# Attention and two MLPs in one planned program: four sums by DMA, a rule for urgent work, other due times, two outputs on a second queue

## The chip, the cores and the metric

The kernel runs on one core of a Trainium2 chip. The metric is the device time of one execution in microseconds (us), the median of three runs for the kernel before. A core has a matrix engine (TensorE, PE in the profile; PEld is its loading of weights), three other engines (VectorE, DVE; ScalarE, ACT; GpSimd, POOL) and SyncE (SP), which here only starts transfers. Each engine works its instructions off in the order in which the program lists them and waits where one needs a result that is not there.

## The reference

All values are fp32. With S = 768 positions, 8 heads of 64, 2 batches (1536 tokens), d_model 512 and d_ff 2048:

```python
def _attn_ref(q, k, v, n_sink, window):          # n_sink 4, window 128
    scores = scale * np.matmul(q, k.transpose(0, 1, 3, 2))
    keep = is_sink | in_window                   # first 4 keys, or the last 128 up to here
    scores = np.where(keep, scores, -1000000000.0)
    a = np.exp(scores - np.max(scores, axis=-1, keepdims=True))
    a = a / (np.sum(a, axis=-1, keepdims=True) + 1e-09)
    return np.matmul(a, v)

def _moe_ref(x, w_in, w_out):
    h = x @ w_in
    return (h * np.clip(h + 3.0, 0.0, 6.0) / 6.0) @ w_out

def _moe2_ref(x, w_in, w_out):
    h = x @ w_in
    return (h * (1.0 / (1.0 + np.exp(-1.702 * h)))) @ w_out

def reference(**kwargs):
    x = attention, with heads put beside each other: (1536, 512)
    return _moe2_ref(_moe_ref(x, moe_w_in, moe_w_out), moe2_w_in, moe2_w_out)
```

## The kernel before

**Arithmetic.** Every fp32 operand of an MLP product is split into a high and a low part (`xy`, `w0h`/`w0l`, `wg`), and a product is three matmuls: high by high, high by low, low by high. The high part is a cast (L444 on ACT, L446 on DVE), the low one a subtraction on DVE (L557 for weights, L572 for the gated values `g`, L1456 for the attention's output x).

**Tiles and stages.** The tokens are 12 tiles of 128. Attention goes by tile and by "duo" (half a tile's heads, 24 duos): 48 score matmuls (L1355), mask and row minimum (L1370, DVE), exponential (L1378, ACT), the inverse of the sums (L1386 and L1387, DVE), four scales (L1397 on DVE or L1395 on ACT, whichever the planner picks), transposes (L1406, 16 for a tile), a copy of what they left (`pts`, L446 or L444), values (L1429 and L1437, 48 for a tile), and the split of x (L444, L1456). An MLP's d_ff is cut into 16 weight tiles f. The packed weights of a tile are loaded by SP (`stage`, two buffers) and converted to fp32 in five steps: L474 on ACT, then L479, L487, L495 and L502 on DVE (the last two 1.2 us each). Up-products (L1132) give h; the gate is L1144 on ACT and L1149 on DVE; down-products are L1181.

MLP1 runs interleaved with attention, in blocks of 512 tokens by 8 weight tiles (first token 0, 512, 512 and 1024), up to about 259 us. The other half of its d_ff, for tokens 0 and 1024, is computed with seven half-size products instead of eight (L717, 336 matmuls of 256 columns; sums around them L734, L741, L750, L755), between about 259 and 325 us, beside MLP2's first block. These products need x in other combinations. `halve` makes them once all attention is done: it adds the high and low part of x back together (L806: two groups of tokens by four tiles = 8 additions of 128x512 on DVE), takes differences (L816) and splits them again (L826, L831). The 8 sums lie in 7 buffers, so the eighth reuses one. What follows, MLP2 in two similar schemes (L629, then L929), is the second half of the run.

**What sets the order.** `Plan.issue` emits the program. Each operation has modelled costs on the engines that may do it, and a due time; due times run backwards from the ends of blocks, whose pace is set by constants (`RAMP0`, `RAMP`, `PAIR`, `PAIR2`, `RATE`, `RATE2`). Of the engine that could start earliest, the planner takes from the operations that could start within `SLACK` = 50 ns of the earliest one the one that is due first:

```python
soon = min(c[0] for c in best[eng]) + SLACK
start, o, cost = min((c for c in best[eng] if c[0] <= soon), key=lambda c: c[1].due)
```

Where an operation may go to two engines, the planner takes the one on which it would end first, with a part of its cost added on each (`PACT` on ACT, `PDVE` on DVE). The order on each engine is fixed by this before the program runs.

**The end.** The last quarter of the output is four pieces, each an addition on DVE (L1052) and a transfer to memory issued by SP (`send`, L978).

Of the kernel before, what the change touches and what calls it, by code (L numbers as in the profile page):

```python
# [9 lines left out]
F32 = mybir.dt.float32  # L10
# [4 lines left out]
ALU = mybir.AluOpType  # L15
# [14 lines left out]
RATE_DMA = 340  # L30
# [3 lines left out]
NVB = 3  # L34
NVC = 3
SLACK = 50
ISSUE = 1300
ADD_DMA = 4500
PACT = 0.15
PDVE = 0.5  # L40
STRETCH = 1.0
LATER = 1000000
H_BANKS = 3
RAMP0 = 9000
RAMP = 1700
PAIR = 4300
PAIR2 = 5500
DOWN = 7000
START = 3000
RATE = 1.6  # L50
RATE2 = 1.25
NU = 3
NG = 2
PX = 8
# [14 lines left out]
def tile_sink_window_attention_moe_moe2(  # L69
# [71 lines left out]
    def load_vc(T):  # L141
# [5 lines left out]
    xyh, xyl = (  # L147
        [
            xy[:, :, (2 * s + k) * NC * 256 : (2 * s + k + 1) * NC * 256].rearrange("p a (c n) -> p a c n", c=NC)
            for s in range(NBLK)  # L150
        ]
        for k in range(2)
    )
# [80 lines left out]
    with tc.tile_pool(name="msk", bufs=1) as mp:  # L234
# [18 lines left out]
            out=out, in0=grid, scalar1=x, scalar2=LOW, op0=op, op1=ALU.mult  # L253
# [41 lines left out]
    class Plan:  # L295
# [70 lines left out]
        def issue(self):  # L366
# [22 lines left out]
            while ready:  # L389
                best = {}  # L390
                for o in ready:
                    placed = self.place(o)
                    if placed is None:
                        continue
                    t = placed[0]
                    pick = None
                    for eng, cost in o.opts:
                        x = max(t, at[eng])
                        for d in o.deps:
                            x = max(x, d.finish + self.lag(d.eng, eng))  # L400
                        score = x + cost * (1 + early[eng])
                        if pick is None or score < pick[0]:
                            pick = (score, x, eng, cost)
                    best.setdefault(pick[2], []).append((pick[1], o, pick[3]))
                assert best, "the plan is stuck"

                eng = min(best, key=lambda e: min(c[0] for c in best[e]))
                soon = min(c[0] for c in best[eng]) + SLACK
                start, o, cost = min((c for c in best[eng] if c[0] <= soon), key=lambda c: c[1].due)
                end = start + cost  # L410
                ready.remove(o)
                for b, n in zip(o.new, self.place(o)[1]):
                    b.slot = n
                    self.slots[b.cls][n] = b
                    b.tile = self.make[b.cls](b.slot)
                o.fn(ENG[eng])
                o.eng = eng
                if eng == "SP":

                    start = max(start, self.lanes.pop(0))  # L420
                    at[eng] = start + 400
                    self.dma_free = max(start + 600, self.dma_free) + cost
                    end = self.dma_free + LAND - 600
                    self.lanes.append(end + 300)
                elif eng == "POOL":
                    at[eng] = start + ISSUE
                else:
                    at[eng] = end
                o.start, o.finish = start, end
                self.end = max(self.end, end)  # L430
                for b in o.bufs:
                    b.left -= 1
                    b.free_at = max(b.free_at, end)
                for b in o.new:
                    if b.kind:
                        self.left[b.kind] -= 1
                for x in succ.get(id(o), ()):
                    need[id(x)] -= 1
                    if not need[id(x)]:
                        ready.append(x)  # L440
# [11 lines left out]
    def parted(x):  # L452

        return x.rearrange("p (a n) -> p a n", a=2)
# [54 lines left out]
    def plan_mlps(plan, blocks, item_due, late=None):  # L509
# [287 lines left out]
        def halve(t0, when):  # L797
# [4 lines left out]
            x = [[b for half in halves(t0, 512) for b in plan.x[half][c]] for c in range(NC)]  # L802
            for c in range(NC):
                plan.op(
                    [("DVE", 602)],
                    lambda e, c=c: e.tensor_tensor(  # L806
                        out=parted(full[c].tile), in0=xyh[s][:, :, c, :].bitcast(F32),
                        in1=xyl[s][:, :, c, :].bitcast(F32), op=ALU.add,
                    ),
                    when, reads=x[c], writes=[full[c]], after=plan.done,  # L810
                )

            def take(a, ac, b, bc, to, tc):
# [46 lines left out]
        def downs(t0):  # L860
# [107 lines left out]
                        when, reads=[x], writes=[y],  # L968
                    )

            def send(to, s, half, when):
                rows = out[s * 512 : s * 512 + 512, :].rearrange("(l q h) d -> q h l d", l=8, q=4)
                share = 4 // len(to)
                for e4 in range(4):
                    y = to[e4 // share]
                    plan.op(
                        [("SP", 131072 / RATE_DMA)],
                        lambda e, e4=e4, y=y: e.dma_start(  # L978
                            out=rows[e4][:, :, half * 256 : half * 256 + 256],
                            in_=y.tile[:, e4 % share * 256 : e4 % share * 256 + 256],  # L980
                        ),
                        when, reads=[y], chain="dma",
                    )
# [65 lines left out]
            for e4 in range(4):  # L1049
# [5 lines left out]
                    ),  # L1055
                    t3, reads=[bw[e4], u4[e4 // 2]], writes=[c12[e4]],
                )
            send(c12, 0, 1, t3)

        def operand(x):  # L1060

# [649 lines left out]
```

## Time and profile before

| | |
|---|---|
| median of 3 runs | 580.94 us (580.4 to 582.3) |
| profiled execution | 582.73 us |
| its span in the profile | 580.86 us |
| busy PE / DVE / ACT / POOL | 97% / 84% / 68% / 9% of the span |
| granted TensorE clock, mean | 0.987 |
| chain that ended last | PE 84%, DVE 10%, ACT 3%, DMA 1% |

The span is the time from the first to the last record of the profile; the 1.87 us around it belong to the execution as well. Busy time of PE is modelled: a matmul of 512 columns is shown as 0.38 us long while the next one starts 0.216 us after it, so a row of PE that reads as busy may still hold short idle times.

### The profile page before, as it was taken

How to read it: one execution, taken by the hardware profiler on the slowest of the kernel's cores; microseconds unless marked ns; L12 is line 12 of the kernel's file. 1: busy time of each engine (PE TensorE's matmuls, PEld its weight loads, DVE VectorE, ACT ScalarE, POOL GpSimd, SP SyncE). 2: the span in 40 equal slices, each digit the busy share in tenths (PEclk: the TensorE clock that was granted, in tenths of full speed). 3: DMA queues.
4: the chain of work that ended last, by engine and by line, in shares of the span. 5: the costliest groups of instructions: out<-in, count | busy, mean ns of one | idle time of the engine just before them, and what ended most of it. 6: DMA issues, size and time to landing. Idle time of an engine off the chain costs nothing.

```text
span 580.9 us, 11878 instructions
## 1 busy us (share of the span) xinstructions
PE 562.5 (97%) x4626; PEld 499.3 (86%) x4626; DVE 489.1 (84%) x1065; ACT 394.0 (68%) x837; POOL 54.1 (9%) x62
## 2 busy tenths in 40 slices
PE   6979999999999999999999999999999999999995
PEld 6858877888878888888999888888888888999995
DVE  6699999999897799999999999997456655667784
ACT  6787857875745667577765736754478788778761
POOL 0000000000000000000000000000003334775000
PEclk9698999999999999999999999999999999999999
DMA  8973464235441000042322132230034477999512
GB/s 261 377 232 114 166 209 160 58 136 187 133 147 73 1 2 0 2 144 78 141 73 77 70 120 83 89 145 1 0 92 72 73 108 138 170 184 199 93 38 77
DMA packets 23471, 65.69 MB, mean 113 GB/s; under 512 B 2480, under 2 KB 10672, under 8 KB 19312
## 3 DMA queue, kind: packets, MB, share of 16 engines
q1 hardware_dynamic: 13360, 51.22, 26.3%
q0 software_dynamic: 10048, 13.63, 14.8%
q8 instruction: 38, 0.62, 0.4%
q14 instruction: 25, 0.20, 0.1%
HBM read 47.02 MB, written 3.15 MB: 86 GB/s over the span
## 4 chain that ended last, share of the span: by engine, by line
PE 84%; DVE 10%; ACT 3%; DMA 1%; issue 1%; POOL 0%; DVEq 0%; POOLq 0%; SPq 0%
PE bank L1181 25%; PE bank L1132 19%; PE bank L929 13%; PE bank L629 13%; PE bank L717 5%; PE bank L1406 3%; PE bank L1355 3%; PE bank L1429 2%; PE bank L1437 1%; DVE wf L495 1%; DVE wf L502 1%; DMA stage<-in_w_dram 1%; DVE pexp L1370 1%; ACT pexp L1378 1%; DVE wf L479 1%
## 5 line engine op out<-in xcount | busy, mean ns | idle before, releaser
L1181 PE MATMUL bank<-wg 128*128 128x512 f32 x768 | 189.3, 382 | 0.4 <-DVE wg L572 0.3
L1181 PEld LDWEIGHTS bank<-wg 128*128 128x128 f32 x768 | 141.6, 189 | 21.0 <-DVE wg L572 2.0
L1132 PE MATMUL bank<-xy,w0h 128*128 128x512 f32 x384 | 117.5, 387 | 2.1 <-ACT xy L444 1.4
L1132 PEld LDWEIGHTS bank<-xy,w0h 128*128 128x128 f32 x384 | 72.0, 191 | 13.3 <-issue 1.5
L1132 PE MATMUL bank<-xy,w0l 128*128 128x512 f32 x192 | 73.5, 383 | 0.1
L444 ACT CAST wg<-wf 128x512 fp32r<-128x512 f32 x81 | 50.2, 621 | 34.5 <-PE bank L1181 26.5
L877 POOL DMA_DIRECT2D wf<-wf x24 | 29.7, 1301 | 467.7 <-ACT wf L858 431.4
L1378 ACT ACTIVATE pexp<-pexp,nb 128x196 f32<-128x196 f32 x96 | 43.1, 453 | 10.3 <-DVE nb L1370 9.9
L557 DVE TENSOR_TENSOR wg<-wf,wg 128x512 fp32r<-128x512 f32 x64 | 44.5, 695 | 5.4 <-ACT wg L444 5.4
L474 ACT ACTIVATE wf<-stage 128x1024 f32<-128x1024 f32 x32 | 37.8, 1182 | 14.6 <-DMA stage<-in_w_dram 13.0
L557 DVE TENSOR_TENSOR w0l<-wf,w0h 128x512 fp32r<-128x512 f32 x60 | 41.6, 693 | 6.5 <-ACT w0h L444 6.4
L1132 PEld LDWEIGHTS bank<-xy,w0l 128*128 128x128 f32 x192 | 36.7, 191 | 5.7 <-DVE w0l L557 0.5
L495 DVE SCALAR_TENSOR_TENSOR wf<-stage,wf 128x1024 int32<-128x1024 int32 x32 | 39.3, 1229 | 0.2
L502 DVE SCALAR_TENSOR_TENSOR wf<-stage,wf 128x1024 int32<-128x1024 int32 x32 | 39.3, 1228 | 0.0
L572 DVE TENSOR_TENSOR wg<-u,wg 128x512 fp32r<-128x512 f32 x56 | 38.7, 694 | 0.1
L1144 ACT ACTIVATE u<-bank,three 128x512 f32<-128x512 f32 x32 | 21.9, 685 | 24.3 <-PE bank L1132 24.2
L629 PE MATMUL bank<-xy,w0h 128*128 128x512 f32 x128 | 38.1, 379 | 0.0
L583 ACT ACTIVATE u<-bank 128x512 f32<-128x512 f32 x32 | 19.1, 596 | 27.2 <-PE bank L1132 20.0
L444 ACT CAST wg<-u 128x512 fp32r<-128x512 f32 x48 | 29.8, 621 | 8.4 <-DVE u L1149 6.3
L1406 PE MATMUL bank<-ident,pexp 128*128 128x128 f32 x192 | 28.3, 288 | 5.1 <-DVE pexp L1397 3.1
L1370 DVE CUSTOM_DVE_ANT_0 pexp<-bank,mask 128x196 f32<-128x196 f32 x96 | 30.2, 356 | 1.6 <-PE bank L1355 1.1
L444 ACT CAST w0h<-wf 128x512 fp32r<-128x512 f32 x49 | 30.2, 615 | 0.9 <-PE bank L629 0.5
(245 smaller groups left out, 1218.5 us busy)
## 6 DMA issues: line engine op xcount, KB each, us to landing
stage<-in_w_dram SPq DMA_DIRECT2D x32, 1024.0 KB, 4.9
wf<-wf POOLq DMA_DIRECT2D x24, 256.0 KB, 3.9
wf<-in_kq_dram SPq DMA_DIRECT2D x8, 520.0 KB, 11.1
vc<-in_vc_dram SPq DMA_DIRECT2D x12, 320.0 KB, 5.5
vb<-in_v_dram SPq DMA_DIRECT2D x10, 256.0 KB, 5.9
kept<-in_kq_dram SPq DMA_DIRECT2D x4, 520.0 KB, 10.9
aside<-wf SPq DMA_DIRECT2D x4, 256.0 KB, 3.9
aside<-wf POOLq DMA_DIRECT2D x4, 256.0 KB, 5.0
```

What stands on the lines that cost most here:

```text
L444: eng.copy(out, in_)
L474: lambda e: e.activation(w.tile.bitcast(F32), top.bitcast(F32), AF.Abs),
L495: lambda e: e.scalar_tensor_tensor(out=w.tile, in0=top, scalar=-0x40000000, in1=w.tile, op0=ALU.bitwise_and, op1=ALU.bitwise_or),
L502: lambda e: e.scalar_tensor_tensor(out=w.tile, in0=low, scalar=29, in1=w.tile, op0=ALU.logical_shift_right, op1=ALU.bitwise_or),
L557: lambda e: e.tensor_tensor(out=lo.tile[at], in0=of(), in1=hi.tile[at].bitcast(F32), op=ALU.subtract),
L572: lambda e: e.tensor_tensor(out=gl.tile, in0=parted(u.tile), in1=gh.tile.bitcast(F32), op=ALU.subtract),
L629: e.matmul(bank.tile, l, woven(r), start=(begin and j == 0 and k == 0), stop=(j == 1 and k == 2), skip_group_check=True,)
L929: e.matmul(to, l, woven(t), start=(begin and n == 0 and m == 0 and e4 % share == 0), stop=(n == pairs - 1 and m == 2), skip_group_check=True,)
L1132: e.matmul(h.tile[:, :n], w, woven(x), start=(c == 0 and k == 0), stop=(c == NC - 1 and k == 2))
L1181: e.matmul(yb.tile, l, woven(r), start=(begin and k == 0), stop=(end is not None and k == 2))
L1378: lambda e, n=n: e.activation(pes[n].tile[:, :W], pes[n].tile[:, :W], AF.Exp, bias=nbs[n].tile, scale=-1.0, accum_out=z.tile[:, n : n + 1],),
L1406: e.transpose(pt.tile[:, n * P : (n + 1) * P], pes[2 * a + j].tile[:, x * P : (x + 1) * P], ident)
```

## The change

Three new constants and a rule: when the operation chosen costs 1000 ns or more (the conversions L495 and L502 on DVE, L474 on ACT, a tile's values on PE, the larger transfers), the planner looks for one that could start within 425 ns more and is due more than 18538 ns earlier, and takes that instead. Seven constants of the due times and costs get other values. The 8 sums of x on DVE become a copy of the low part by a DMA on SP (L812 of the changed kernel) and an accumulating DMA of the high part on POOL (L817). The last four outputs alternate between SP and ACT.

```diff
+HOLD = 425
+MARGIN = 18538
+LONG = 1000
...
-PACT = 0.15
+PACT = 0.1
...
-RAMP0 = 9000
-RAMP = 1700
+RAMP0 = 7993
+RAMP = 1510
...
                 start, o, cost = min((c for c in best[eng] if c[0] <= soon), key=lambda c: c[1].due)
+                if cost >= LONG:
+                    sooner = [c for c in best[eng] if c[0] <= soon + HOLD and c[1].due < o.due - MARGIN]
+                    start, o, cost = min(sooner, key=lambda c: c[1].due, default=(start, o, cost))
...
             for c in range(NC):
                 plan.op(
-                    [("DVE", 602)],
-                    lambda e, c=c: e.tensor_tensor(
-                        out=parted(full[c].tile), in0=xyh[s][:, :, c, :].bitcast(F32),
-                        in1=xyl[s][:, :, c, :].bitcast(F32), op=ALU.add,
+                    [("SP", 262144 / RATE_DMA)],
+                    lambda e, c=c: e.dma_start(out=parted(full[c].tile), in_=xyl[s][:, :, c, :].bitcast(F32)),
+                    when, reads=x[c], writes=[full[c]], after=plan.done,
+                )
+                plan.op(
+                    [("POOL", ADD_DMA)],
+                    lambda e, c=c: e.dma_start(
+                        out=parted(full[c].tile), in_=xyh[s][:, :, c, :].bitcast(F32), accum_op=ALU.add
                     ),
-                    when, reads=x[c], writes=[full[c]], after=plan.done,
+                    when, reads=x[c], writes=[full[c]],
                 )
...
-            def send(to, s, half, when):
+            def send(to, s, half, when, issuers=("SP",)):
...
-                        [("SP", 131072 / RATE_DMA)],
+                        [(by, 131072 / RATE_DMA if by == "SP" else ISSUE)],
...
-            send(c12, 0, 1, t3)
+            send(c12, 0, 1, t3, ("SP", "ACT"))
```

Lines of the changed kernel stand 6 to 11 higher than those of the kernel before (L1397 becomes L1408, L495 becomes L501, L1395 becomes L1406).

**First place: attention's sixth tile.** On DVE of the kernel before, these are the inverses and scales (L1386, L1387, L1397) of the tile's two duos, between conversions of a weight tile, a gate and a split:

```order
L1397 TENSOR_SCALAR pexp<-pexp,z 128x196 x4
L487 TENSOR_SCALAR wf<-wf 128x1024
L557 TENSOR_TENSOR wg<-wf,wg 128x2x256
L1386 TENSOR_SCALAR z<-z 128x4
L1387 RECIPROCAL z<-z 128x4
L1149 SCALAR_TENSOR_TENSOR u<-u,bank 128x512
L1397 TENSOR_SCALAR pexp<-pexp,z 128x196 x2
L495 SCALAR_TENSOR_TENSOR wf<-stage_60,wf 128x1024
L572 TENSOR_TENSOR wg<-u,wg 128x2x256
```

On DVE of the changed kernel the scales of the same tile are L1408; two are left there, one of them here and one in the row right behind these:

```order
L493 TENSOR_SCALAR wf<-wf 128x1024
L1408 TENSOR_SCALAR pexp<-pexp,z 128x196
L501 SCALAR_TENSOR_TENSOR wf<-stage_60,wf 128x1024
L1397 TENSOR_SCALAR z<-z 128x4
L1398 RECIPROCAL z<-z 128x4
L508 SCALAR_TENSOR_TENSOR wf<-stage_60,wf 128x1024
```

On ACT of the changed kernel the rest of the tile's scales are L1406, around the conversion L480:

```order
L1406 ACTIVATE pexp<-pexp,z 128x196
L1389 ACTIVATE pexp,z<-pexp,nb 128x196
L1406 ACTIVATE pexp<-pexp,z 128x196 x2
L480 ACTIVATE wf<-stage_61 128x1024
L1406 ACTIVATE pexp<-pexp,z 128x196 x3
L1155 ACTIVATE u<-bank,three 128x512
```

Six of the tile's eight scales stood on DVE before; two stand there now, and six on ACT. Over the whole of attention it is 68 on DVE and 28 on ACT before, 56 and 40 now.

**Second place: after the last tile.** On DVE of the kernel before, four of the eight sums (L806) follow the last split of x (L1456), with the first difference (L816):

```order
L1456 TENSOR_TENSOR xy<-bank,xy 128x4x128
L806 TENSOR_TENSOR vb_63<-xy 128x512
L806 TENSOR_TENSOR vb_64<-xy 128x512
L1149 SCALAR_TENSOR_TENSOR u<-u,bank 128x512
L557 TENSOR_TENSOR w0l<-wf,w0h 128x512
L557 TENSOR_TENSOR wg<-wf,wg 128x2x256
L572 TENSOR_TENSOR wg<-u,wg 128x2x256
L806 TENSOR_TENSOR vb_65<-xy 128x512
L806 TENSOR_TENSOR vc_66<-xy 128x512
L816 TENSOR_TENSOR vb_63<-vb_63 128x2x128
```

On SP of the changed kernel the eight copies (L812) stand between two loads of weights for MLP2:

```order
L123 DMA stage_60<-in_w_dram 128x2048
L123 DMA stage_61<-in_w_dram 128x2048
L812 DMA vb_64<-xy 128x2x256
L812 DMA vc_66<-xy 128x2x256 x2
L812 DMA vc_67<-xy 128x2x256 x2
L812 DMA vc_68<-xy 128x2x256 x2
L812 DMA vc_66<-xy 128x2x256
L123 DMA stage_60<-in_w_dram 128x2048
```

On POOL of the changed kernel the eight accumulating transfers (L817) are the first work, ahead of those of the later stages (L887):

```order
L817 DMA vb_64<-xy 128x2x256
L817 DMA vc_66<-xy 128x2x256 x2
L817 DMA vc_67<-xy 128x2x256 x2
L817 DMA vc_68<-xy 128x2x256 x2
L817 DMA vc_66<-xy 128x2x256
L887 DMA wf<-wf 128x2x256 x2
```

The sums leave DVE; SP's queue gets eight transfers that wait for the last tile, the eighth also for a buffer, with a load of weights behind it; POOL's gets eight that wait each for its copy.

**Third place: the end.** SP's last rows of the kernel before (L1638 is the program's end):

```order
L978 DMA out_dram<-u 16x8x256 x4
L978 DMA out_dram<-vb_65 16x8x256 x2
L978 DMA out_dram<-vc_67 16x8x256 x2
L978 DMA out_dram<-u 16x8x256 x4
L978 DMA out_dram<-stage_60 16x8x256 x2
L978 DMA out_dram<-stage_61 16x8x256 x2
L1638 UNCONDITIONAL_BRANCH
```

SP's last rows of the changed kernel:

```order
L989 DMA out_dram<-u 16x8x256 x4
L989 DMA out_dram<-vc_66 16x8x256 x2
L989 DMA out_dram<-vb_65 16x8x256 x2
L989 DMA out_dram<-u 16x8x256 x4
L989 DMA out_dram<-stage_60 16x8x256
L989 DMA out_dram<-stage_61 16x8x256
L1649 UNCONDITIONAL_BRANCH
```

ACT's last rows of the changed kernel:

```order
L969 ACTIVATE vc_68<-bank 128x512 x2
L897 ACTIVATE wg<-vb_64 128x2x256
L450 CAST wg<-wf 128x2x2x128
L897 ACTIVATE w0h<-vc_67 128x512
L450 CAST wg<-wf 128x2x2x128
L989 DMA out_dram<-stage_60 16x8x256
L989 DMA out_dram<-stage_61 16x8x256
```

Of the last four outputs, two stay on SP and two come last on ACT, behind its last work.

## Rows read from the trace of the kernel before

**Rows 1.** Stretches: us; busy PE, PEld, DVE, ACT, POOL (instructions); PEclk; DMA share; GB/s.

```profile
13.10:23.35 10.25, 9.84 (x152) 8.61 (x154) 6.46 (x33) 8.40 (x24) 0.00 (x0) 0.50 1.03 350
...
43.82:47.25 3.43, 3.43 (x8) 2.79 (x9) 3.40 (x17) 3.31 (x10) 0.00 (x0) 0.50 0.85 316
47.25:109.28 62.03, 60.30 (x678) 50.73 (x677) 59.47 (x153) 46.30 (x111) 0.00 (x0) 1.00 0.42 135
109.28:205.00 95.72, 95.36 (x1008) 81.60 (x1008) 84.34 (x203) 60.16 (x144) 0.00 (x0) 1.00 0.33 111
205.00:258.80 53.80, 53.80 (x252) 47.12 (x251) 53.46 (x99) 36.36 (x65) 0.00 (x0) 1.00 0.11 40
258.80:324.95 66.15, 65.10 (x457) 60.53 (x457) 65.98 (x134) 46.55 (x100) 0.00 (x0) 1.00 0.27 96
324.95:574.40 249.45, 249.44 (x1476) 226.10 (x1475) 187.34 (x306) 168.03 (x304) 52.71 (x52) 1.00 0.47 96
```

**Rows 2.** Chain that ended last: start us, us, engine and line.

```profile
126.87 1.75 PE bank L1406 x16
...
141.38 0.86 PE bank L1355 x48
...
212.18 2.59 PE bank L1132 x12
...
499.35 75.05 PE bank L929 x672
```

**Rows 3.** The same chain around the values of the last tile.

```profile
201.60 0.37 PE bank L1429 x4
...
203.56 0.63 PE bank L1132 x2
```

**Rows 4.** Waits from 47.25 to 109.28: engine line <- releaser: us, times, longest.

```profile
PEld bank L1355 <- DVE u L1149: 1.4, 1, 1.4
...
PEld bank L1132 <- DVE w0l L557: 0.5, 1, 0.5
```

**Rows 5.** Waits from 109.28 to 205.

```profile
PEld bank L1181 <- DVE wg L572: 1.2, 2, 0.7
```

**Rows 6.** Waits from 258.8 to 324.95.

```profile
PEld bank L717 <- DVE u L741: 1.4, 2, 0.8
```

**Rows 7.** VectorE forms: xcount | busy us, mean ns | idle before, releaser.

```profile
L502 DVE SCALAR_TENSOR_TENSOR wf<-stage,wf 128x1024 int32<-128x1024 int32 x32 | 39.3, 1228 | 0.0
...
L479 DVE TENSOR_SCALAR wf<-wf 128x1024 f32<-128x1024 f32 x32 | 22.1, 697 | 0.5 <-ACT wf L474 0.5
...
L1397 DVE TENSOR_SCALAR pexp<-pexp,z 128x196 f32<-128x196 f32 x68 | 18.2, 318 | 0.1
...
L446 DVE CAST w0h<-wf 128x512 fp32r<-128x512 f32 x11 | 4.7, 423 | 0.0
...
L446 DVE COPY pts<-bank 128x512 f32<-128x512 f32 x6 | 4.1, 687 | 1.6 <-PE bank L1406 1.6
...
L806 DVE TENSOR_TENSOR vc<-xy 128x512 f32<-128x512 f32 x4 | 2.7, 687 | 0.0
```

**Rows 8.** A scale on ScalarE, same columns.

```profile
L1395 ACT ACTIVATE pexp<-pexp,z 128x196 f32<-128x196 f32 x28 | 12.0, 456 | 1.6 <-DVE z L1387 1.5
```

**Rows 9.** Issues of accumulating transfers on GpSimd, same columns.

```profile
L877 POOL DMA_DIRECT2D wf<-wf x24 | 29.7, 1301 | 467.7 <-ACT wf L858 431.4 <-DMA wf<-wf 14.4 <-DVE wg L912 11.6
```

**Rows 10.** Transfers: queue xcount, KB each, median us from issue to landing.

```profile
wf<-wf POOLq DMA_DIRECT2D x24, 256.0 KB, 3.9
...
wf<-vc POOLq DMA_DIRECT2D x4, 256.0 KB, 11.7
...
out_dram<-stage SPq DMA_DIRECT2D x4, 128.0 KB, 3.8
```

**Rows 11.** SyncE's queue at the end: start us, us, what.

```profile
573.54 2.65 SPq L978 DMA_DIRECT2D out_dram<-stage  x3
```

**Rows 12.** The last sum on VectorE.

```profile
574.43 0.42 DVE L1052 TENSOR_TENSOR stage<-bank,vc 128x256 f32<-128x256 f32 x1 [0.24 <-PE bank L929]
```

More of the change, by code (lines that the diff above doesn't have):

```diff
@@ L43 @@
 H_BANKS = 3
-RAMP0 = 9000
-RAMP = 1700
-PAIR = 4300
-PAIR2 = 5500
+RAMP0 = 7993
+RAMP = 1510
+PAIR = 4538
+PAIR2 = 5889
 DOWN = 7000
 START = 3000
-RATE = 1.6
-RATE2 = 1.25
+RATE = 1.61
+RATE2 = 1.21
 NU = 3
@@ L975, in send @@
                     y = to[e4 // share]
+                    by = issuers[e4 % len(issuers)]
                     plan.op(
-                        [("SP", 131072 / RATE_DMA)],
+                        [(by, 131072 / RATE_DMA if by == "SP" else ISSUE)],
                         lambda e, e4=e4, y=y: e.dma_start(
```

## The prediction

> **What bounds the kernel now.** I read the table by stretches first. From 324.95 to 574.40 PE is busy 249.44 of 249.45 us [rows 1]: only its own work counts there, and the change touches none of it before the very end. So the change can act in attention, in the half-size products, and in the tail.
>
> A busy PE in this view hides short gaps, so for the earlier stretches I compare the length with the work: number of matmuls times pitch. The pitches come from pieces of the chain in which PE waited for nothing [rows 2, 3]: 2.59/12 = 0.216 us for a matmul of 512 columns, 75.05/672 = 0.112 for one of 256, 0.86 for the scores of a duo, 1.75/16 = 0.109 for a transpose, 203.56 - 201.60 = 1.96 for the values of a tile.
>
> - 47.25 to 109.28, with the 3.43 us before it [rows 1]: 65.5 us. Their matmuls (678 in the row, a few records missing) are 189 of 512 columns, 6 duos' scores, 64 transposes and 3 tiles' values: 40.8 + 5.2 + 7.0 + 5.9 = 58.9. Lost: 6.6 us.
> - 109.28 to 258.80: 149.5 us for 567 matmuls, 8 duos, 64 transposes, 5 tiles (1008 + 252 in the rows): 122.4 + 6.9 + 7.0 + 9.8 = 146.1. Lost: 3.4.
> - 258.80 to 324.95: 66.15 us for 336 of 256 columns and 120 of 512 (457): 37.5 + 25.9 = 63.4. Lost: 2.7.
>
> Two stretches were granted a clock of 0.50, which is 1.2 GHz: 10.25 us from 13.10 and the 3.43 us from 43.82 [rows 1]. The second costs 1.7 of the 6.6.
>
> Then the waits: who was late? In the first of these stages PE's weight loads waited 1.4 us for DVE's gate L1149 and 0.5 for the low part of a weight, L557 [rows 4]; in the second 1.2 for DVE's L572 [rows 5]; in the third 1.4 for DVE's L741 [rows 6]. DVE is the late engine each time, and it is busy 59.47 of 62.03, 84.34 of 95.72, 53.46 of 53.80 and 65.98 of 66.15 us, while ACT's share is 63 to 75% [rows 1]. So the change is worth what it takes off DVE ahead of those waits.
>
> **The change part by part.** I count DVE's instructions in the order ahead of a given operation, at the same PE work done, before and now, and price them by busy time over count [rows 7]: a scale 18.2/68 = 0.27 us, a cast of weights 0.43, a copy of transposes 0.69, a sum of x 0.68, L479 (and L487, its like) 0.69, L502 1.23.
>
> *Start, up to 47 us.* Ahead of the first up-product DVE has one scale and one copy fewer and two row minima, one cast and two splits more; PE gets one duo's scores earlier. The signs are mixed: 0, between -2 and +2 (either stretch at 1.2 GHz could move: they follow idle PE, and half of 3.43 is 1.7).
>
> *First stage.* Ahead of the eighth down-product: 11 scales and one copy fewer (-3.0, -0.7), two casts and one split more (+0.9, +0.7, the split by the price of a copy): -2.1. The waits that name DVE are 1.4 + 0.5 = 1.9, less than that, so they go: -1.9. What follows them is ACT, which takes the scales, and ACT's shorter share covers it. Ends: -3.5 (the 6.6 less the clock's 1.7, and 1.4 for the gate's own chain), and +1 if the wait on ACT replaces it.
>
> *Second stage.* Twelve scales and four copies have left DVE (-3.2, -2.8), conversions are held back behind more urgent work (one each of L479, L487, L502 not yet done: -2.6), five weight casts and two casts of `wg` more (+3.0), and the eight sums are gone (-5.4): together -11.0 ahead of the first half-size product's addition. Only 1.2 us of PE's loss names DVE: -1.2, between 0 and -2.8. The held-back conversions are no gain by themselves; they must still run, and here they do so later.
>
> *The rule for urgent work and the due times* do not remove work. Attention ends later in the new order: 54 more matmuls of 512 columns stand ahead of the last tile's values, 54 x 0.216 = 11.7 us. That costs nothing while the sums of x, which start from there, are ready in time (third rival).
>
> *Half-size products.* DVE reaches them with those 11 us less behind it, and after 24 of the additions 16 less. The loss is 2.7, of which 1.4 names DVE; half of the rest likely hangs on it through ACT's gates, which waited for the same additions: -2.0, between 0 and -2.7.
>
> *Sums by DMA.* The copies go behind the weight loads on SP, and a load of MLP2 weights stands behind the eighth; the adds go to POOL, which is idle (x0) up to 324.95 [rows 1]. A transfer of 256 KB on POOL's queue landed in 3.9 us in the common case and in 11.7 in the slowest row [rows 10]; POOL's issues took 1.30 each [rows 9]. With x complete at about 215 us (203.56, where the last tile's values end now [rows 3], plus 11.7): copies at 219, seven adds issued by 228, landed by 232; the eighth sum, whose buffer has to come free, about 235. That is 20 us ahead of the half-size products, so I cost it at 0. Cover gone, see below.
>
> *Tail.* SP's last three issues stretch over 2.65 us from 573.54, to 576.19 [rows 11], while the last sum ends at 574.43 + 0.42 = 574.85 [rows 12]: 1.34 us of queueing. With every other one on ACT, the last issue starts at 574.85, behind nothing. No row shows an issue on ACT; the nearest are the mean of SP's three, 0.88, and POOL's 1.30 [rows 9]: it would end at 575.73 or 576.15. I take SP's, the queue that does the same transfer: -0.5. Ends: -1.3 (all of the queueing goes) and +1.5 (a slow issue, and a landing later than the 3.8 of [rows 10]).
>
> Sum: 0 - 1.9 - 1.2 - 2.0 - 0.5 = -5.6. The profiled execution took 582.73, so a like one would take 577.1; it lay 1.8 above the median of the runs, 580.94, and the prediction for the median is 580.94 - 5.6 = **575.3 us**. All ends at once would be -12.3 and +4.5.
>
> **The rivals.**
>
> *ACT takes over.* It gets 12 scales at 12.0/28 = 0.43 [rows 8], 5.1 us, and four copies, some 2.7, in attention. If ACT then is late for the gates, the first two stages gain nothing: -2.0 - 0.5 = -2.5, 578.4 us. For it: ACT's scales cost more than DVE's 0.27. Against: ACT is busy 60.16 of 95.72 us [rows 1]. 0.12.
>
> *The gain does not come, except at the end.* PE's waits for DVE are replaced by others of like length (a chain of mask, exponential, inverse, scale is as long as before), and only the tail is left: 580.4, no change that can be told. 0.08.
>
> *The sums come too late.* This is the one that makes it slower. The chain is copy, add, difference, copy, add: four landings for the eighth sum, of which each must follow the last. At 11.7 us each it is 215 + 46.8 + about 2 of issues = 264, where the first products that need them run at about 254: PE has nothing else for up to 10 us, and the weight load behind the eighth copy is late with it. That is 575.3 + 10 = 585.3. It decides from landings of about 9.3 us ((254 - 215 - 2)/4). For it: a row of POOL's queue lands that late. Against: DMA share is 0.11 from 205 to 258.8, where the copies are, and 0.47 where the rows of 11.7 stand [rows 1, 10]. 0.10.
>
> The Trainium skill ("SBUF — State Buffer", section "SBUF: two separate sides") has a rule that speaks for this rival: a DMA issued by GpSimd needs its descriptors written, and cannot get them while VectorE runs an operation that takes the port pair both share, such as an fp32 copy or an operation with a scalar. DVE is 99% busy in that stretch, and L479 is such an operation. No row here separates it. By it each of the eight adds would wait for up to one L479 of 0.69 us, an estimate of 5.5 us spread over the eight; by the rows, none. By it the chance of this rival would be above the 0.10 that the rows give, and the sum the same, against 20 us of slack.
>
> **How the numbers follow.** My forecast holds 0.70, ACT 0.12, nothing 0.08, late sums 0.10. Around 575.3 the forecast itself runs from 570 to 579. A measurement of this kernel tells differences from about 0.3%, 1.74 us: 579.2 to 582.7 is "same". ACT's case at 578.4 is mostly faster. So faster: 0.68 + 0.10 = 0.78; same: 0.08 + 0.03 = 0.11; slower: 0.10 + 0.01 = 0.11. The range reaches to the case of no gain and leaves out the late sums: 570.0 to 581.0.
>
> **What would show it.** DVE's L806 rows gone, two rows on SP and POOL of 8 each, landing near 4 us, and no long wait ahead of the differences (L816) that follow them. In the waits, the rows with L1149, L572 and L741 ahead of PE's weight loads shorter by about 1.9, 1.2 and 1.4; the half-size products in about 64 us instead of 66.15; scales 56 on DVE and 40 on ACT; the last issue about 0.9 us after the last sum, not 1.34. The prediction is wrong if PE's waits for DVE stay as long (then order, not DVE's load, set them), if ACT's gates show up as PE's releaser in attention, if the clock is at 1.2 GHz for longer than 10.25 + 3.43 us, or if the takes wait for the sums.

## The result: 573.2 us, and where the profile after has the time

| | before | after |
|---|---|---|
| median (runs beside each other) | 581.10 us (6 runs, 580.1 to 582.3) | 573.17 us (6 runs, 572.3 to 574.3) |
| ratio of the times | 1 | 0.9864, 95% interval 0.9849 to 0.9879 |
| profiled execution, its span | 582.73, 580.86 us | 572.57, 570.8 us |

The change gains 7.9 us by the medians; 5.6 were forecast, and the range (570.0 to 581.0) holds the time. The two profiled executions lie 10.2 us apart: before's was 1.6 above its median and after's 0.6 below. So I compare the stages of more than these two executions below.

The stretches of the profile after, cut where PE had done as much work as at the cuts of [rows 1] (5.78, 43.82, 109.28, 205, 258.80 and 324.95 us); columns as there:

```profile
5.40:40.71 35.31, 28.45 (x747) 24.63 (x751) 31.23 (x135) 29.74 (x101) 0.00 (x0) 0.90 0.99 324
40.71:103.85 63.14, 61.31 (x685) 52.19 (x681) 62.35 (x164) 54.36 (x135) 0.00 (x0) 1.00 0.47 155
103.85:197.81 93.96, 93.96 (x942) 81.04 (x944) 82.80 (x189) 55.85 (x128) 3.82 (x3) 1.00 0.41 127
197.81:252.20 54.39, 54.39 (x329) 47.63 (x321) 48.69 (x101) 39.73 (x79) 6.17 (x5) 1.00 0.31 72
252.20:316.21 64.01, 64.01 (x457) 60.47 (x456) 62.24 (x126) 45.23 (x98) 0.00 (x0) 1.00 0.24 83
316.21:565.64 249.43, 249.42 (x1477) 226.49 (x1475) 193.49 (x314) 171.22 (x308) 52.59 (x52) 1.00 0.50 104
```

Against the stretches of before: 38.0 us have become 35.3 and 65.5 have become 63.1 (the cut between these two is rough, since scores now stand ahead of the first up-product), 149.5 have become 148.4, and the half-size products 64.0 instead of 66.15. The last long stretch is unchanged, and 1.3 us went from the tail. In the second row, DVE is busy 62.35 of 63.14 us; in the two stretches of before that hold the same work of PE it was busy 3.40 + 59.47 of 65.46 us [rows 1]. So DVE's idle time fell from 2.6 to 0.8 us: DVE stays nearly full in this stage, before and after.

The forms that the change moved, from the profile after (DVE, then ACT; L1408 and L1406 are the scales, L452 the cast of [rows 7]):

```profile
L1408 DVE TENSOR_SCALAR pexp<-pexp,z 128x196 f32<-128x196 f32 x56 | 15.0, 318 | 0.1
...
L452 DVE CAST w0h<-wf 128x512 fp32r<-128x512 f32 x16 | 6.7, 422 | 1.2 <-PE bank L1143 1.0
```

```profile
L1406 ACT ACTIVATE pexp<-pexp,z 128x196 f32<-128x196 f32 x40 | 16.2, 452 | 1.8 <-DVE z L1398 1.8
```

Counts and prices are as counted in the order. What the prediction left out is a wait on ACT. In the profile before, between 72 and 83 us (start, duration, engine, line; in brackets the idle time ahead and what ended it):

```profile
72.23 1.22 DVE L502 SCALAR_TENSOR_TENSOR wf<-stage,wf 128x1024 int32<-128x1024 int32 x1
...
73.53 0.33 SPq L120 DMA_DIRECT2D stage<-in_w_dram  x1
...
80.23 1.15 ACT L474 ACTIVATE wf<-stage 128x1024 f32<-128x1024 f32 x1 [3.22 <-DMA stage<-in_w_dram]
81.28 0.67 ACT L1144 ACTIVATE u<-bank,three 128x512 f32<-128x512 f32 x1
...
81.98 0.69 DVE L1149 SCALAR_TENSOR_TENSOR u<-u,bank 128x512 f32<-128x512 f32 x1 [1.41 <-ACT u L1144]
...
82.72 0.32 PE L1355 MATMUL bank<-wf 64*64 64x64 f32 x2 [0.97 <-DVE u L1149]
```

Read downwards: DVE ends the last step of one conversion (L502) at 73.45, which frees one of the two weight buffers; SP issues the next load at 73.53; ACT stands in front of that load, in L474, and does nothing for 3.22 us; the gate L1144 behind it is late, so is DVE's half of the gate, and so are the scores. The wait on DVE that I had found in [rows 4] is the last link of this. In the profile after, the same conversion, load and start:

```profile
65.70 1.20 DVE L508 SCALAR_TENSOR_TENSOR wf<-stage,wf 128x1024 int32<-128x1024 int32 x1
...
66.97 0.33 SPq L123 DMA_DIRECT2D stage<-in_w_dram  x1
...
71.95 1.19 ACT L480 ACTIVATE wf<-stage 128x1024 f32<-128x1024 f32 x1 [1.01 <-DMA stage<-in_w_dram]
...
77.76 0.66 ACT L1155 ACTIVATE u<-bank,three 128x512 f32<-128x512 f32 x1
```

(L123 is L120 of the kernel before.) The conversion ends 6.6 us earlier (2.4 of them because the kernel is that far ahead there), the load with it, and no gate stands right behind L480. ACT's waits for loads in this stage, from the table of waits of before (47.25 to 109.28) and of after (47 to 103):

```profile
ACT wf L474 <- DMA stage<-in_w_dram: 5.6, 3, 3.2
```

```profile
ACT wf L480 <- DMA stage<-in_w_dram: 1.2, 2, 1.0
```

From this comes the theory that I tested against the prediction's: the *buffer theory* says that time in attention goes where an in-order engine stands in a long conversion or in front of a late load, with urgent work behind it; the *DVE theory* is the prediction's, that the gain is the amount of work taken off DVE.

### The profile page after: what moved, and what is told of

Its sections match the earlier page's. It is cut to its first block, busy times and chain, and to the rows that moved or that the text cites. A ratio compares the mean times of both kernels' runs of the same rounds, so it can differ in the third digit from the quotient of the medians.

```text
span 570.8 us, 11900 instructions
## 1 busy us (share of the span) xinstructions
PE 555.3 (97%) x4626; PEld 496.0 (87%) x4626; DVE 483.1 (85%) x1045; ACT 398.0 (70%) x849; POOL 64.0 (11%) x70
## 3 DMA queue, kind: packets, MB, share of 16 engines
q0 software_dynamic: 12224, 15.73, 17.5%
## 4 chain that ended last, share of the span: by engine, by line
PE 90%; DVE 4%; DMA 2%; issue 1%; SPq 1%; ACT 0%
PE bank L1192 29%; PE bank L1143 21%; PE bank L939 13%; PE bank L635 13%; PE bank L723 7%; PE bank L1417 3%; PE bank L1366 2%; DMA wf<-in_kq_dram 2%; PE bank L1440 1%; PE bank L1448 1%; DVE wf L501 1%; DVE pexp L1381 1%; DVE wf L508 1%; DVE pexp L1408 0%; DVE wf L493 0%
## 5 line engine op out<-in xcount | busy, mean ns | idle before, releaser
L887 POOL DMA_DIRECT2D wf<-wf x24 | 29.0, 1301 | 228.5 <-ACT wf L868 193.1
L480 ACT ACTIVATE wf<-stage 128x1024 f32<-128x1024 f32 x32 | 37.8, 1183 | 7.9 <-DMA stage<-in_w_dram 7.9
L501 DVE SCALAR_TENSOR_TENSOR wf<-stage,wf 128x1024 int32<-128x1024 int32 x32 | 39.1, 1223 | 0.1
L1417 PEld LDWEIGHTS bank<-ident,pexp 128*128 128x128 f32 x192 | 24.0, 151 | 6.8 <-issue 2.5
```

Of the source, the lines that this page charges most:

```text
L501: lambda e: e.scalar_tensor_tensor(out=w.tile, in0=top, scalar=-0x40000000, in1=w.tile, op0=ALU.bitwise_and, op1=ALU.bitwise_or),
L1417: e.transpose(pt.tile[:, n * P : (n + 1) * P], pes[2 * a + j].tile[:, x * P : (x + 1) * P], ident)
```

## Experiments: single rows moved

For these three, the order of the kernel before was written out as a table of its 2482 decisions and played back, which gives its order row for row; then one row was moved (r_gate), two (r_conv) or four (r_scale). (Line numbers stand 99 higher in them: L573 is L474, L1248 is L1149, L1454 is L1355, L1280 is L1181.)

**r_gate.** ACT's order, one row moved:

```diff
-ACTIVATE wf<-stage_60 128x1024
 ACTIVATE u<-bank,three 128x512
+ACTIVATE wf<-stage_60 128x1024
```

The gate L1144 now stands ahead of the conversion's start L474.

> The kernel before, its order written out row by row, with one row moved: on ACT the start of a weight conversion (L474, which at 80.23 us had waited 3.22 us for its load) stands behind the next gate (L1144) instead of ahead of it. Buffer theory (in attention ACT stands in front of a weight load that comes late, and the gate behind it makes DVE and then PE wait): PE's gap of 1.13 us at 81.4 us closes, the time falls by 1.0 to 1.7 us. DVE theory (the time lost there is DVE's amount of work, as the prediction had it): DVE's work is untouched, so no change beyond 0.3 us.

Measured 579.93 us, ratio 0.9979 (0.9963 to 0.9996). On ACT, its trace has the gate first, 1.3 us earlier than at 81.28, and the load's wait gone from this place:

```profile
79.96 0.69 ACT L1243 ACTIVATE u<-bank,three 128x512 f32<-128x512 f32 x1 [3.04 <-PE bank L1231]
80.64 1.18 ACT L573 ACTIVATE wf<-stage 128x1024 f32<-128x1024 f32 x1
```

By the ratio that is 1.2 us of 581, as the buffer theory had it, with DVE's work untouched; PE's gap of 1.13 us in front of the scores is 0.1 in this trace. The interval runs from 0.2 to 2.1 us, so the 0.3 that the DVE theory allowed lies at its edge.

**r_conv.** DVE's order, two rows moved up:

```diff
 TENSOR_SCALAR wf<-wf 128x1024
+SCALAR_TENSOR_TENSOR wf<-stage_60,wf 128x1024
+SCALAR_TENSOR_TENSOR wf<-stage_60,wf 128x1024
 TENSOR_TENSOR wg<-wf,wg 128x2x256
 ...
 SCALAR_TENSOR_TENSOR u<-u,bank 128x512
 TENSOR_SCALAR pexp<-pexp,z 128x196 x2
-SCALAR_TENSOR_TENSOR wf<-stage_60,wf 128x1024
 TENSOR_TENSOR wg<-u,wg 128x2x256
-SCALAR_TENSOR_TENSOR wf<-stage_60,wf 128x1024
```

> The kernel before, its order written out, with two rows moved: on DVE the last two steps of one weight conversion (L495, L502) stand right behind its L487 and ahead of a weight split, a gate, six scales and a split of g. Buffer theory: the buffer comes free about 2.5 us earlier (73.45 us before), the load lands so much earlier, ACT's wait of 3.22 us falls under 1 us, and the time falls by 1.0 to 1.7 us, less what the gate that now stands 2.3 us later on DVE costs. DVE theory: the same work in another order with the gate later, no gain, up to 2 us slower.

Measured 583.97 us, ratio 1.0050 (1.0027 to 1.0073): slower. Waits of its trace from 47.25 to 109.28:

```profile
ACT wf L573 <- DMA stage<-in_w_dram: 2.1, 2, 1.3
...
PE bank L1454 <- DVE u L1248: 1.7, 1, 1.7
...
PE bank L1280 <- DVE wg L656: 0.5, 1, 0.5
```

The first half of the buffer theory's expectation came true: ACT's waits for loads fell from 5.6 to 2.1 us, and the one of 3.22 us is gone. The gain did not come: the gate behind two conversions of 1.2 us made PE wait 1.7 us there, and more followed. The sign is the one that the DVE theory had, and 2.9 us is more than its 2 (the interval, 1.6 to 4.2 us, holds both). So a weight buffer that comes free earlier is worth nothing if its conversion then stands in front of a gate. In r_gate and r_conv the amount of DVE's work is that of before; what moved the time is the order.

**r_scale.** Four scales (`L1397`) of the sixth tile put on ACT (`L1395`).

> The kernel before, its order written out, with four of the six scales that the sixth attention tile has on DVE put on ACT, as the changed kernel has them, and nothing else. DVE theory: 4 x 0.27 = 1.1 us less DVE work ahead of the late rows, so about 1.0 us faster. Buffer theory: the buffer comes free 1 us earlier, ACT's wait falls from 3.2 to about 2.2 us, 0.4 to 1.0 us faster. A rival (ACT is the bound): 4 x 0.43 = 1.7 us more on ACT, slower by up to 1 us.

Measured 580.92 us, ratio 0.9997 (0.9980 to 1.0014). Neither theory's gain shows; a gain of 1.0 us as the DVE theory had it is near the edge of the interval. ACT's waits for loads were 4.8 us, where before had 5.6 and b_tail, with the same order in this stage, 4.4.

**b_pact.** The kernel before with `PACT = 0.1`: ten scales go to ACT, due times as before.

> The kernel before with only the weight on ACT changed (0.15 to 0.1): ten scales go from DVE to ACT (58 and 38), DVE has 1 us less to do ahead of the eighth down-product and 1.8 us less ahead of the half-size products. DVE theory: 1 to 2 us faster. Theory of the order (what counts is where conversions stand, and so when their buffers come free): within 0.3% of the kernel before, since the due times are as before.

Measured 582.07 us, ratio 1.0013 (0.9988 to 1.0037): no gain on the whole, where the DVE theory had 1 to 2 us. But these runs had less of TensorE's clock than those of before beside them (median of the mean granted clock 0.985 against 0.989; the profiled execution 20.4 us at 0.50 up to 50 us, before 13.7). The eight executions below 0.988 took 582.0 to 584.9 us, the four at 0.988 and above 578.9 to 580.2. Whether the new order draws the slower clock, or chance did, no run tells. So b_pact does not take the scales away as a cause, and r_scale excludes no more than a gain above 1.2 us.

## Experiments: the parts one by one

The parts are four: the seven constants, the rule, the sums by DMA (eight of them, four for each of two groups of tokens), and the tail on ACT. Each was put alone into the kernel before, or taken alone out of the changed kernel. The planner then writes a new order for what follows, and that belongs to what is measured: in b_sums, DVE's order is another one from its 529th instruction on.

**b_tail**, the tail alone:

```diff
-            send(c12, 0, 1, t3)
+            send(c12, 0, 1, t3, ("SP", "ACT"))
```

> The kernel before with only the last four outputs alternating between SP and ACT. The prediction's term: 0.5 us faster. What the trace of the changed kernel shows between its last sum and the end of the span (4.7 us against 6.0): 1.3 us faster. Rival (the last landing sets the end whoever issues it): no change.

Measured 581.31 us, 0.9997: nothing that can be told; the 1.3 us of the trace are excluded by the interval, the 0.5 of the prediction is not.

**b_sums**, the sums alone:

```diff
-                    [("DVE", 602)],
+                    [("SP", 262144 / RATE_DMA)],
...
+                    [("POOL", ADD_DMA)],
```

> The kernel before with only the sums of x by DMA. DVE theory: 3.3 us less DVE work at the first half-size addition and 6 us less at the last: the loss of 2.7 us in the half-size products falls by 1.0 to 2.0, all else as before. Rival (sums come late, or the transfers ahead of a weight load hold it up): 0 to 10 us slower.

Measured 582.03 us, 1.0019: the eight sums are gone from DVE, and the kernel is slightly slower (0.2 to 2.0 us). Against the DVE theory, inside the rival's range.

**b_due**, the constants alone:

```diff
-PACT = 0.15
+PACT = 0.1
...
-RAMP0 = 9000
+RAMP0 = 7993
...
```

> The kernel before with only the seven constants changed (due times and the weight on ACT). Up to the eighth down-product its order on DVE is that of the changed kernel (scales 56 on DVE, 40 on ACT). DVE theory, by the prediction's terms: -1.9 ahead of that product, part of -1.2 behind it, and in the half-size products nearly all of -2.0 (9 of the 11 us of DVE work are gone there): 4 to 5 us faster. Rival (the rule for urgent work makes the gain): under 2 us faster.

Measured 578.02 us, 0.9951: 2.8 us, between the two expectations. By the table below the first stage gains 3.0 to 4.8 us and the stages behind it lose some of that again. ACT's waits for loads from 47.25 to 109.28 fell to 0.9 us.

**b_rule**, the rule alone:

```diff
+                if cost >= LONG:
+                    sooner = [c for c in best[eng] if c[0] <= soon + HOLD and c[1].due < o.due - MARGIN]
+                    start, o, cost = min(sooner, key=lambda c: c[1].due, default=(start, o, cost))
```

> The kernel before with only the rule for urgent work. It changes the order from the eleventh weight conversion on; ahead of the half-size products DVE has 1.8 us less to do, at their end 5 us less. DVE theory: nothing up to the eighth down-product, -0.5 to -1.5 in all after it. Rival (the rule makes the gain): 4 us faster or more.

Measured 581.04 us, 1.0007: no gain; the 0.5 of the DVE theory is at the edge of the interval.

**a_nosums**, the changed kernel with the eight sums on DVE as before:

```diff
-                    [("SP", 262144 / RATE_DMA)],
+                    [("DVE", 602)],
...
```

> The changed kernel with the sums of x on DVE again. DVE theory: at the first half-size addition DVE has done 222.6 us of work where PE has done 227, so DVE is still ahead and the sums cost nothing by now: within 0.5 us of the changed kernel, about 573 to 574 us, a ratio of 0.986 to 0.988 to the kernel before. Rival (the sums' time on DVE is what the half-size products waited for): 1.5 to 2 us slower than the changed kernel, 575.

Measured 574.07 us, 0.9889: 0.9 us slower than the changed kernel by the medians, 1.5 by the ratios, between the two expectations; the interval (0.9867 to 0.9910) holds both.

**a_norule**, the changed kernel without the three lines of the rule:

```diff
-                if cost >= LONG:
...
```

> The changed kernel without the rule for urgent work. The constants alone gave 2.9 us of the 7.9, the rule alone nothing. If the parts add up (sums 1, tail 0.5): 4.3 us faster than before, ratio 0.9925. If the rule works only with the new due times (the two together gave 6.6 with the tail): 3 to 4.5 us slower than the changed kernel. If the rule does nothing at all and the sums and the tail make up the rest: as fast as the changed kernel, 0.9865.

Measured 578.45 us, 0.9952: 5.3 us slower than the changed kernel and no faster than b_due. The parts don't add up; even more hangs on the rule than the second case had.

**a_oldconst**, the changed kernel with the old constants:

```diff
-RAMP0 = 7993
+RAMP0 = 9000
...
```

> The changed kernel with the seven constants of the kernel before (rule, sums and tail stay). Due-time theory (the constants move the conversions and so the weight loads in attention): the loss between the first up-product and the eighth down-product comes back, 4 us, and the half-size products lose over 2 us again: ratio 0.995 to 1.0. Rival (the rule finds the urgent work whatever the due times): 0.99 or below.

Measured 579.54 us, 0.9977: the due-time theory's range.

**a_notail**, the changed kernel with the old tail:

```diff
-            send(c12, 0, 1, t3, ("SP", "ACT"))
+            send(c12, 0, 1, t3)
```

> The changed kernel with all of the last four outputs on SP again. The prediction's term: 0.5 us slower than the changed kernel. From the profiles that have the old tail (6.0, 5.4, 6.0, 6.0 us behind the last matmul against 5.3 and 5.4 with the new one): 0.3 to 0.7 us slower. Rival (nothing to be had): within 0.2.

Measured 573.78 us, 0.9882: 0.6 us slower than the changed kernel, the size expected, but the interval (0.9857 to 0.9907) holds 0.9864 too.

| kernel | parts in it | median, us | ratio to before (95%) |
|---|---|---|---|
| b_tail | tail | 581.31 | 0.9997 (0.9981 to 1.0014) |
| b_sums | sums | 582.03 | 1.0019 (1.0004 to 1.0034) |
| b_rule | rule | 581.04 | 1.0007 (0.9992 to 1.0022) |
| b_due | constants | 578.02 | 0.9951 (0.9929 to 0.9973) |
| a_norule | constants, sums, tail | 578.45 | 0.9952 (0.9937 to 0.9967) |
| a_oldconst | rule, sums, tail | 579.54 | 0.9977 (0.9959 to 0.9995) |
| a_nosums | constants, rule, tail | 574.07 | 0.9889 (0.9867 to 0.9910) |
| a_notail | constants, rule, sums | 573.78 | 0.9882 (0.9857 to 0.9907) |
| the changed kernel | all | 573.17 | 0.9864 (0.9849 to 0.9879) |

The parts don't add up. Alone, three of them gain nothing or lose, and the constants gain 2.8 us. Taken out of the whole, the constants cost 6.4 us, the rule 5.3, the sums 0.9 and the tail 0.6 (differences of medians; for the last two the intervals overlap that of the changed kernel). Constants and rule together make 6.6 of the 7.9, with the tail.

Where each works is seen in PE's lost time by stage: from the starts of the matmuls in each trace, the time between points of equal PE work, less that work, by the pitches of [rows 2, 3] (us; one execution each).

| stage, by PE work done | before | b_tail | r_scale | b_rule | a_oldconst | b_due | a_norule | a_nosums | after |
|---|---|---|---|---|---|---|---|---|---|
| first up-product to 8th down-product (22 to 80) | 9.7 | 8.7 | 8.7 | 8.8 | 9.6 | 4.9 | 4.9 | 4.9 | 4.9 |
| to the half-size products (80 to 227) | 4.0 | 3.6 | 3.2 | 3.1 | 2.9 | 4.5 | 4.5 | 2.9 | 2.9 |
| half-size products (227 to 285) | 2.8 | 2.7 | 2.7 | 3.1 | 2.8 | 3.4 | 4.0 | 2.0 | 0.7 |
| behind the last matmul | 6.7 | 5.4 | 6.0 | 6.0 | 5.0 | 6.1 | 5.1 | 5.2 | 5.3 |

The first row belongs to the constants alone: every kernel with them has 4.9, and every one with the old ones 8.0 (b_sums) to 9.7, apart from r_conv with 11.3. Two places in it can be named. In front of the scores behind the gate of 81.28 us, at 57 to 60 of PE's work, the untouched old order loses 0.6 to 1.8, r_gate 0.4, and every kernel with the new constants 0.3. A little later, at 62 to 65, every kernel with the old constants except b_pact loses 1.3 to 1.4, and those with the new ones 0.2: transposes wait there for a copy on ACT, which stands behind a conversion's start, two scales and a gate. Rows of before:

```profile
87.22 1.17 ACT L474 ACTIVATE wf<-stage 128x1024 f32<-128x1024 f32 x1
...
89.56 2.02 ACT L444 COPY pts<-bank 128x512 f32<-128x512 f32 x4
...
90.19 0.66 PE L1406 MATMUL bank<-ident,pexp 128*128 128x128 f32 x4 [0.59 <-ACT pts L444]
```

Only the first place was tested by moving a row (r_gate). b_pact loses 0.3 and 0.2 at the two places although its waits for loads there still sum to 4.1 us, so a scale's engine and the order that follows from it can clear them without an earlier load. Which of the seven constants counts, and how much of the 3.0 to 4.8 us hangs on the late loads, is not shown.

The amount of DVE's work stays a rival for this row. From 22 to 80 of PE's work, first in b_sums (whose order up to there is that of before), then in after:

```profile
39.90:105.30 65.40, 61.70 (x712) 51.99 (x709) 64.32 (x175) 49.55 (x124) 0.00 (x0) 1.00 0.48 161
```

```profile
39.20:101.60 62.40, 60.57 (x713) 51.90 (x710) 61.61 (x165) 53.51 (x135) 0.00 (x0) 1.00 0.48 160
```

DVE is busy 64.32 of 65.40 us and 61.61 of 62.40, so it has 2.7 us less to do in a stage that is 3.0 us shorter: ten scales fewer, and the last two steps of one weight tile are done ahead of the stage. r_scale and b_pact took only some 0.5 us off DVE's busy time there, less than their intervals can tell.

The rule has its effect in the next two rows when the new constants are there: without it they lose 4.5 and 4.0, with it 2.9 and 2.0, and the sums then take 2.0 to 0.7. With the old constants the second row is as low with the rule (3.1 and 2.9) as b_pact has it without (2.9), and the third hardly moves (3.1 and 2.8). The trace of a_norule shows what the rule moves away. Its waits in the half-size products (255 to 322 us):

```profile
ACT wf L477 <- DMA stage<-in_w_dram: 2.8, 3, 1.4
...
PEld bank L720 <- ACT u L737: 1.2, 1, 1.2
PEld bank L720 <- DVE u L744: 1.1, 3, 0.7
PEld bank L720 <- ACT vb L737: 0.9, 2, 0.7
```

and two places of its timeline, ACT's rows and the matmul that waits for them:

```profile
267.03 1.17 ACT L477 ACTIVATE wf<-stage 128x1024 f32<-128x1024 f32 x1 [1.36 <-DMA stage<-in_w_dram]
...
278.20 1.16 ACT L477 ACTIVATE wf<-stage 128x1024 f32<-128x1024 f32 x1
279.26 0.36 ACT L737 COPY vb<-bank 128x256 f32<-128x256 f32 x1
...
279.68 0.49 PE L720 MATMUL bank<-xt,sh 128*128 128x256 f32 x2 [0.55 <-ACT vb L737]
```

At 278.20 ACT takes 1.16 us for the start of a conversion, and the short copy that PE needs stands behind it. The five starts of conversions from 250 us on lie at 253.7 to 300.1 us here; in after, with the rule, they lie at 263.7 to 318.0. There the same stretch (252 to 317) has no wait of ACT for a load and one small one of PE's:

```profile
PEld bank L723 <- ACT vb L740: 0.2, 1, 0.2
```

So these rows agree with the buffer theory: the rule keeps conversions from standing in front of short urgent work. That is read from two traces; no single row was moved here. Why the rule alone (b_rule) gained nothing stays open.

## Why the prediction was right, point by point

- *Start, 0 forecast.* 18.2 us were lost up to the first up-product before, 17.5 after; 0.7 better, inside the bounds.
- *First stage, -1.9 forecast.* This term was mis-sized. The profiled pair shows -4.8, the other executions with the old order -3.0 to -4.8. The prediction took the waits that name DVE [rows 4] as the price ("the waits that name DVE are 1.4 + 0.5 = 1.9, less than that, so they go"). They did not all go: of 1.9 us, 1.2 still name DVE in after, in other places (47 to 103 us), while the transposes' wait for ACT's copy, left out of the price, fell from 0.8 to 0.2 (first row before, the rest after):

```profile
PEld bank L1406 <- ACT pts L444: 0.8, 1, 0.8
```

```profile
PEld bank L1192 <- DVE u L1160: 0.7, 1, 0.7
PEld bank L1143 <- DVE w0l L563: 0.5, 1, 0.5
...
PEld bank L1417 <- ACT pts L450: 0.2, 1, 0.2
```

  The waits that name DVE were thus not the price. One of them came from ACT in front of a late load (r_gate, 1.2 us); the copy behind a conversion's start is another 1.1; how much of the rest is DVE's amount of work is open, and so is what the scales are worth. I had a row of 5.6 us of ACT's waits for loads in the same table and did not follow who stood behind it.
- *Second stage, -1.2 forecast.* -1.1 in the pair, and between nothing and -1.1 over the executions (3.2 to 4.0 before, 2.9 to 3.3 after). The wait that names L572 fell from 1.2 to 0.3 us. Size right; which part makes it is not told apart, since kernels with the rule alone or with `PACT` alone have 3.1 and 2.9 as well.
- *The rule and the due times "do not remove work".* True, and the wrong thing to conclude from: by the ratios, without the rule 2.8 us of the gain are left, without the constants 1.3.
- *Half-size products, -2.0 forecast.* 2.77 to 0.74: -2.0. Of this the sums are 1.3 in the traces, once constants and rule are there. Alone they are worth nothing (b_sums), and b_due, in which 9 of the "11 us less behind it" are gone too, lost 3.4 in this stage: the amount by itself was not the reason.
- *Sums in time.* They were. The rows of after for seven of the eight copies and adds:

```profile
vc<-xy SPq DMA_DIRECT2D x7, 256.0 KB, 2.6
vc<-xy POOLq DMA_DIRECT2D x7, 256.0 KB, 4.7
```

  The copies start on SP and the last add on POOL at (two rows of the timeline):

```profile
184.46 0.69 SPq L812 DMA_DIRECT2D vb<-xy  x1
...
230.20 1.22 POOL L817 DMA_DIRECT2D vc<-xy  x1 [12.91 <-DVE xt L841]
```

  The first tokens' copies did not wait for the last tile, which I had put at 215. The eighth add, issued at 230.20, landed by about 236 (none of the eight took more than 5.9 us), where 235 was worked out; the half-size products start at 252. The rule that I cited from the Trainium skill ("SBUF — State Buffer", section "SBUF: two separate sides"), by which VectorE can hold up the descriptors of a transfer issued by GpSimd, has no row here that shows it or rules it out: the adds landed in 3.7 to 5.9 us while DVE was busy 90% of the stretch, where a like transfer took 3.9 before [rows 10].
- *Tail, -0.5 forecast.* 0.6 by a_notail against the changed kernel, within its interval, and nothing that can be told by b_tail. The profiled pair's 1.3 is mostly luck of the execution of before: the kernels with the old tail have 5.4 to 6.7 us behind the last matmul. ACT's issues took about 0.6 us, less than POOL's 1.30 [rows 9], as the end of after shows (last sum on DVE, ACT's queue):

```profile
565.67 0.42 DVE L1063 TENSOR_TENSOR stage<-bank,vc 128x256 f32<-128x256 f32 x1 [0.24 <-PE bank L939]
```

```profile
564.79 1.90 ACTq L989 DMA_DIRECT2D out_dram<-stage  x2
```

  The sum ends at 566.09 and the last issue at 566.69: 0.60 us behind the sum, where it was 1.34.
- *The rivals.* ACT did not take over with 12 more scales; its share stayed under 87%. The sums were not late. That PE's waits for DVE are replaced by others of like length was half right for the first stage (1.2 of 1.9 us still name DVE), but it did not mean that nothing is gained.

The sign and the range were right, the size 5.6 for 7.9. That the total came out this near is partly luck: in the first stage and in the half-size products the reason given, the amount of work taken off DVE, is not what the runs show to be decisive, and the prices happened to be of the right order.

## What to carry to other kernels

When a wait names an engine, follow it back through that engine's own wait until a transfer or a full buffer is met: the row to price is the first late thing, not the last link. On engines that work in order, a long instruction or one that may have to wait for a load belongs behind the short ones that others wait for (r_gate gained 1.2 us by that), and early enough that its buffer is free for the next load; the second without the first lost 2.9 us (r_conv). Parts of a planner's change need not add up: the rule was worth nothing alone and 5.3 us beside the constants. Judge a term of 1 us from several executions of the same order, with the granted clock of each beside it, before it is explained.

## What the runs showed that was not expected

The half-speed stretches of TensorE's clock are not tied to the order of the program. Before had 10.25 us at 0.50 from 13.10 and 3.43 us from 43.82 [rows 1]; r_scale, the same order up to 65 us, in the same windows:

```profile
13.10:23.35 10.25, 10.25 (x164) 8.92 (x164) 6.54 (x33) 8.45 (x25) 0.00 (x0) 0.56 1.03 350
43.82:47.25 3.43, 3.43 (x17) 3.00 (x17) 3.40 (x18) 3.41 (x11) 0.00 (x0) 1.00 0.90 331
```

The second stretch is missing there. The first lies about 1 us earlier (hence 0.56), and where it is missing nothing is gained: b_tail, with 3.4 us at 0.50 from 28.0 in its place, lost 18.8 us up to the first up-product, before 18.2 and r_scale 18.0. The DMA share is 1.03 in that window, which may be why; no run tests it. In the second place the half-speed stretch is worth about 0.9 us (3.5 against 2.6 lost in the first up-product), where the prediction had put it at 1.7. The profiled execution of the changed kernel had two stretches of 3.4 us there, 6.8 us in place of 13.7. Such differences, and a load that took 6.7 us from its issue to ACT's start in one execution, are of the size to matter in the 5 us between the fastest and the slowest of 35 runs of the kernel before (578.6 to 583.8), and in the 2 us by which the profiled pair overstates the gain; what makes these up was not followed.

The executions of b_tail and a_nosums took 1.90 to 2.13 us outside their span (medians 2.04 and 2.06), those of the other kernels, the changed one with the same tail among them, 1.73 to 1.93. What this hangs on stays open; of the 0.9 us that a_nosums lost by the medians, 0.3 lie there.
